# A reordered head: filter loads, the first query tile, evictions and the banks of the first scores

## The chip, the cores and the metric

The kernel runs on 1 core of one Trainium2 chip. The time is what the device takes for one execution of the program, in microseconds (us); a lower time is better. Three runs of the kernel before gave 633.48, 634.38 and 632.29 us, and the profiled execution, a fourth one, took 633.24 us.

## The reference, cut to what matters

Two branches read inputs of their own, and their outputs stand side by side. Branch A is attention with 16 query heads of 28 numbers that share one head of keys and values, over 2048 positions. Branch B is a two-dimensional Fourier filter of a 2048 x 448 array.

```python
def _A_ref(x, wq, wk, wv, wo):
    q = (x @ wq).reshape(B, S, H, Dh).transpose(0, 2, 1, 3)      # H = 16, Dh = 28
    k, v = x @ wk, x @ wv
    scores = jnp.einsum("bhqd,bkd->bhqk", q, k) * (Dh ** -0.5)
    o = jnp.einsum("bhqk,bkd->bhqd", _softmax(scores, axis=-1), v)
    return o.transpose(0, 2, 1, 3).reshape(B, S, H * Dh) @ wo

def _B_ref(x, w_r, w_i):
    X = jnp.fft.rfft2(x, axes=(-2, -1)) * (w_r + 1j * w_i)
    return jnp.fft.irfft2(X, s=(S, D), axes=(-2, -1))

return jnp.concatenate([_A_ref(...), _B_ref(...)], axis=-1)
```

## The kernel before, in words

**Two stages.** The head computes queries, keys and values and the first half of the Fourier transform. The loop after it computes 1024 tiles of scores (128 keys by 512 queries), their exponentials, the sums over values, the output projection, and the rest of the Fourier branch in between.

**The projection in the head.** The input comes in four chunks of 512 positions (`xa` into `raw`). Each number is split into a high part and a remainder, so that fast matmuls keep the precision. `group(n)` (L431) runs the matmuls (L369) of one chunk and one group of heads; the result is copied from PSUM to `qraw` on ScalarE (L373), and VectorE takes its largest magnitude (`qmx`, L374). Four spare rows of each head's 32 carry the keys and values along. `fetch` (L274) gathers the keys into `kf`, `fetch_v` (L280) the values into `vt`.

**The keys.** `keys(h)` makes one half of the key operand `ka`: ScalarE copies the high part (L287), VectorE subtracts it for the remainder `kl` (L288), and three DMAs (L293) fill the other 96 rows: high once more, and the remainder twice. Every score matmul has 128 rows: high and remainder of the query against high and remainder of the key.

**The first query tile.** A score tile needs `qa[0, 0]`. Its chain is: `qmx` times the largest key (`terms`, L296), a small matmul that adds it up per head (`shift`, L301), a copy to `cvec` (L302), the shifted query `ql` (VectorE, L232), its high part `qh` (ScalarE, L229), the remainder (VectorE, L218), and 16 copies `copy_q` of 32 rows each: rows 0 to 31 of the four heads by VectorE (L205), rows 32 to 63 by ScalarE (L203), rows 64 to 95 by DMAs of SP, and rows 96 to 127 by DMAs of POOL (both L206). The first score tile reads head 0, the second head 1, and so on.

**The Fourier half in the head.** For each of eight pieces q, SP loads `xb` (512 KB, L120) and the table `fw` (128 KB, L124). `fft1_fold` (L129 to L134) forms sums on VectorE, `fft1_a` multiplies (L155) and copies out `a` on ScalarE (L144), `fft1_b` multiplies `a` by `fw` (L172), copies the result to `bs` (L180 on ScalarE for q below 6, L182 on VectorE for 6 and 7), and stores it to the DRAM tensor `t1` with two DMAs (`t`, L185). Buffers are reused: the `xb` of piece q + 4 is loaded once `fft1_a(q)` has read it.

**What sets the order.** TensorE, VectorE and ScalarE run in the order of the program text (for the last two from `group(4)` on); SP and POOL issue DMAs in the order shown below. Each engine works through its queue in order. In the loop a table (`PLAN`) and a small clock model choose which instruction comes next. After the head, `free` lists six PSUM banks in the order in which the first scores take them; two banks that the last Fourier piece used and that of the maximum check `pb3` (L503, L504) are among them. From then on a step of the loop is four score tiles (L917), four exponentials (L852 or L928 on ScalarE), and four matmuls with the values (L863).

**After the head.** `fft2_load` (L588) reads `t1` back once all 16 stores have landed, and only behind it on SP's queue come the copies of the second query tile (L223, L225). POOL loads the filter weights `wr`, `wi` (L593).

Of the kernel before, what the change touches and what calls it, by code (L numbers as in the profile page):

```python
# [10 lines left out]
F32 = mybir.dt.float32  # L11
# [4 lines left out]
ALU = mybir.AluOpType  # L16
# [6 lines left out]
DF = D // 2 + 1  # L23
# [49 lines left out]
def kernel(ctx: ExitStack, tc: tile.TileContext, t: dict):  # L73
    nc = tc.nc
# [4 lines left out]
    fp = ctx.enter_context(tc.tile_pool(name="fp", bufs=2))  # L79
# [8 lines left out]
    ka = cp.tile([128, S], F32R, name="ka")  # L88
# [4 lines left out]
    t1 = dp.tile([64, 64, DF], F32, name="t1")  # L93
# [10 lines left out]
    def aux2(name):  # L104
        return aux_pool[0].tile([128, 2, DF], F32, name=name, tag="aux")
# [9 lines left out]
    def fft1_load(q, parts=(0, 1)):  # L115
        if q > 7:
            return
        if 0 in parts:
            x = fp.tile([128, 4, 256], F32, name="xb", tag=("wr", "b2")[q % 2])
            nc.sync.dma_start(x, t["xb"][q])  # L120
            xb[q] = [x, None]
        if 1 in parts:
            w = xb[q][1] = fp.tile([128, 4, 64], F32, name="fw", tag=("ph", "pl")[q % 2])
            nc.sync.dma_start(w, t["fw"][:, 4 * q:4 * q + 4])  # L124

    def fft1_fold(q):
        x = xb[q][0][:113]
        f = fp.tile([113, 4, 256], F32, name="f", tag="wi")
        nc.vector.tensor_tensor(f[:, 0:2], x[:, 0::2], x[:, 1::2], op=ALU.add)  # L129
# [7 lines left out]
    at1, stored = {}, []  # L137

    def fft1_a(*qs):
        for q in qs:  # L140
            for p in range(2):
                pa = fft1_a_mm(q, p)
                a = at1[q, p] = fp.tile([128, 2, DF], F32, name="a", tag=("pwr", "pwi")[p])
                nc.scalar.activation(a, pa, AF.Copy)  # L144
            fft1_load(q + 4, (0,))
# [18 lines left out]
    def fft1_mm(q, pb=None):  # L164
        w = xb[q][1]
        if pb is None:
            pb = aux2("pbb"), ps_o.tile([128, 2, DF], F32, name="po")
        for p in range(2):
            a = at1.pop((q, p))
            for h in range(2):  # L170
                for e in range(2):
                    mm(pb[h][64 * e:64 * e + 64, p], w[64 * h:64 * h + 64, 2 * p + e], a[64 * h:64 * h + 64, e],  # L172
                       start=True, stop=True)
        return pb

    def fft1_out(q, pb):
        bs = fp.tile([128, 2, 2, DF], F32, name="bs", tag="cst" if q < 6 else "b2")
        for h in range(2):
            if q < 6:
                nc.scalar.activation(bs[:, h], pb[h], AF.Copy)  # L180
            else:
                nc.vector.tensor_copy(bs[:, h], pb[h])  # L182
        for e in range(2):
            n0 = 16 * e + 2 * q
            stored.append(nc.sync.dma_start(t1.rearrange("s (l n) f -> s l n f", l=2)[:, :, n0:n0 + 2],  # L185
                                            bs[64 * e:64 * e + 64]))

    def fft2_consts():
        for n in ("g1", "g2"):
# [9 lines left out]
    def copy_q(i, p, q, src, eng):  # L199

        o, x = q[32 * p:32 * p + 32, i], src[32 * i:32 * i + 32].bitcast(F32)
        if eng is nc.scalar:
            return eng.activation(o, x, AF.Copy)  # L203
        if eng is nc.vector:
            return eng.tensor_copy(o, x)  # L205
        return eng.dma_start(o.bitcast(F32), x)  # L206

    def build_q(c, g, first=False):
        cs = slice(c * CW, (c + 1) * CW)
        qh = qp.tile([128, CW], F32R, name="qh", bufs=1)  # L210
        ql = qp.tile([128, CW], F32R, name="ql", bufs=1)
        qt = ql.bitcast(F32)
        if (c, g) not in qa:
            qa[c, g] = qp.tile([128, 4, CW], F32R, name="qa")
        q = qa[c, g]

        def split():
            nc.vector.tensor_tensor(ql, qt, qh.bitcast(F32), op=ALU.subtract)  # L218
# [6 lines left out]
            nc.sync.dma_start(q[64:128].bitcast(F32), q[0:64].bitcast(F32))  # L225

        def high():
            if first:
                return nc.scalar.activation(qh, qt, AF.Copy)  # L229
            return nc.vector.tensor_copy(qh, qt)  # L230

        ops = [(540, lambda: nc.vector.tensor_scalar(qt, qraw[:, g, cs], mask, cvec[:, g, c:c + 1],  # L232
                                                     op0=ALU.mult, op1=ALU.add)),
               (450, high), (710, split)]
        if not first:
            return ops
        for _, op in ops:
            op()
        return q, qh, ql
# [3 lines left out]
    ps_o = ctx.enter_context(tc.tile_pool(name="ps_o", bufs=O_BUFS, space=PSUM))  # L243
# [3 lines left out]
    free = deque(ps_s.tile([128, 512], F32, name=f"s{i}") for i in range(BANKS))  # L247

    def bank():
        free.rotate(-1)  # L250
        return free[-1]

    def pair_of(b):
        return b[:, :2 * DF].rearrange("p (n f) -> p n f", n=2)


    with tc.tile_pool(name="w1", bufs=1) as w1:
# [24 lines left out]
        def keys(h):  # L282
            hs = slice(h * 1024, h * 1024 + 1024)
            kl = w1.tile([32, 1024], F32R, name="kl")
            src = kf[:, hs].rearrange("p (s t j) -> p s t j", s=2, j=32)
            high = ka[:32].rearrange("p (t s j) -> p s t j", s=NC, j=32)[:, 2 * h:2 * h + 2]
            nc.scalar.activation(high, src, AF.Copy)  # L287
            nc.vector.tensor_tensor(kl.rearrange("p (t s j) -> p s t j", s=2, j=32), src, high.bitcast(F32),  # L288
                                    op=ALU.subtract)
            kt = ka.rearrange("p (t x) -> p t x", t=16)[:, :, 64 * h:64 * h + 64]  # L290
            low = kl.rearrange("p (t x) -> p t x", t=16)
            for p, src in ((1, kt[:32]), (2, low), (3, low)):
                nc.sync.dma_start(kt[32 * p:32 * p + 32].bitcast(F32), src.bitcast(F32))  # L293
# [11 lines left out]
        with tc.tile_pool(name="x1", bufs=2) as x1:  # L305
# [151 lines left out]
            for j in range(NK):  # L457
                split_x(*xs[3], 3, j)
            group(5)
            keys(0)  # L460
# [33 lines left out]
        copy_q(1, 1, qf, ql, nc.scalar)  # L494
        fft1_a(6, 7)
# [5 lines left out]
        fft1_b(6, 7)  # L501
        for g in range(NG):
            mm(pb3[0:1, 4 * g:4 * g + 4], cmax[:, g:g + 1], sel4, start=True, stop=True)  # L503
        nc.vector.tensor_reduce(bits, pb3[0:1, 0:16], axis=AX.X, op=ALU.max)  # L504
# [76 lines left out]
    b2 = {}  # L581
# [14 lines left out]
    pr, cst = {}, {}  # L596
# [245 lines left out]
    kept, po = [], {}  # L842
# [341 lines left out]
```

## Time and profile before

| | |
|---|---|
| median of three runs | 633.48 us (632.29 to 634.38) |
| profiled execution | 633.24 us, of which the span from the first to the last instruction is 631.5 us |
| TensorE clock granted | 1.0 over the whole span |
| HBM traffic | 29.77 MB read, 17.87 MB written, 75 GB/s over the span |
| first score matmul | starts 68.17 us after the span's start |
| first exponential of a score | starts at 68.76 us |

The timeline's rows give start, duration, engine (PE is TensorE, DVE VectorE, ACT ScalarE; SPq and POOLq are the issuing queues), line, output and inputs, count, and in brackets the idle time ahead of the row with what ended it. A matmul's record ends some time after the next one has begun, since they are pipelined: 512 columns start 0.23 us apart though one lasts 0.39 us. The time of a DMA row is that of its issue, not of its transfer.

### The profile page before, as it was taken

Reading aid. Unit: us, or ns where it says so; the run is one execution under the profiler, and the core shown is the slowest. Engines: PE = TensorE matmul, PEld = TensorE weight load, DVE = VectorE, ACT = ScalarE, POOL = GpSimd, SP = SyncE. Lnnn points to the kernel's source line nnn. Section 1 sums busy time; section 2 is a strip of 40 time slices with the busy share of each in tenths; the row PEclk is TensorE's granted clock in tenths of the full one; section 3 lists DMA queues with packets and bytes.
Section 4 is the critical chain, followed back from the end, with each engine's and each line's share of the span. In section 5 each row is a group of like instructions: output and inputs, shape, how many; then the busy total and the mean of one; then the engine's idle time right before and its main releaser. Section 6 shows DMA issues by size and latency. Waiting matters only on the chain. (4 is left out here: it accounts for less than half of the span.)

```text
span 631.5 us, 12130 instructions
## 1 busy us (share of the span) xinstructions
PE 625.5 (99%) x4420; PEld 377.6 (60%) x4420; DVE 430.2 (68%) x775; ACT 547.2 (87%) x986; POOL 67.4 (11%) x132
## 2 busy tenths in 40 slices
PE   9999999999999999999999999999999999999997
PEld 7888545655555556646555665555556565555555
DVE  5996458779999944857766845277687764457753
ACT  5565999999999998988899989999989989989991
POOL 3522211011203110000110100001010100000000
PEclk9999999999999999999999999999999999999999
DMA  8857773446456523126340513034152413030001
GB/s 255 290 162 199 215 181 99 103 132 184 121 156 144 149 56 83 59 70 184 80 113 6 128 35 82 16 84 147 42 122 60 111 46 89 16 82 15 17 30 62
DMA packets 40931, 66.71 MB, mean 106 GB/s; under 512 B 11189, under 2 KB 25926, under 8 KB 39904
## 3 DMA queue, kind: packets, MB, share of 16 engines
q1 hardware_dynamic: 35232, 52.50, 30.4%
q0 software_dynamic: 5056, 12.45, 7.6%
q8 instruction: 36, 0.59, 0.4%
q10 hardware_dynamic: 576, 0.92, 0.4%
q14 instruction: 31, 0.25, 0.1%
HBM read 29.77 MB, written 17.87 MB: 75 GB/s over the span
## 5 line engine op out<-in xcount | busy, mean ns | idle before, releaser
L852 ACT ACTIVATE p<-s 128x512 f32<-128x512 f32 x392 | 217.8, 646 | 24.9 <-PE s L917 23.9
L917 PE MATMUL s<-qa,ka 128*128 128x512 f32 x736 | 222.6, 402 | 0.0
L917 PEld LDWEIGHTS s<-qa,ka 128*128 128x128 f32 x736 | 134.5, 188 | 58.6 <-issue 26.2
L863 PE MATMUL s<-p,vs 128*32 128x512 f32 x1144 | 141.7, 595 | 0.0
L923 DVE COPY k<-s 128x512 f32<-128x512 f32 x119 | 78.2, 685 | 68.1 <-PE s L917 67.9
L942 ACT ACTIVATE k<-k 128x1024 f32<-128x1024 f32 x80 | 83.4, 1140 | 0.0
L852 ACT ACTIVATE qraw<-s 128x512 f32<-128x512 f32 x136 | 78.0, 646 | 2.3 <-PE s L917 2.3
L863 PEld LDWEIGHTS s<-p,vs 128*32 128x32 f32 x1144 | 34.3, 109 | 76.2 <-issue 69.7
L852 ACT ACTIVATE p<-po 128x512 f32<-128x512 f32 x88 | 57.2, 650 | 6.5 <-PE po L917 6.4
L917 PE MATMUL po<-qa,ka 128*128 128x512 f32 x151 | 60.9, 404 | 0.0
L917 PE MATMUL sx<-qa,ka 128*128 128x512 f32 x137 | 55.2, 403 | 0.0
L863 PE MATMUL s<-qraw,vs 128*32 128x512 f32 x424 | 54.8, 593 | 0.0
L863 PE MATMUL s<-k,vs 128*32 128x512 f32 x352 | 46.3, 594 | 0.0
L852 ACT ACTIVATE p<-sx 128x512 f32<-128x512 f32 x64 | 42.0, 656 | 3.0 <-PE sx L917 2.9
L738 POOL DMA_DIRECT2D ol<-ol x36 | 18.0, 508 | 229.3 <-DVE ol L761 157.2
L867 DVE STREAM_TRANSPOSE osb<-s 128x512 f32<-128x512 f32 x15 | 10.7, 716 | 38.9 <-PE s L863 38.8
L917 PEld LDWEIGHTS po<-qa,ka 128*128 128x128 f32 x151 | 28.4, 188 | 13.6 <-issue 6.7
L917 PEld LDWEIGHTS sx<-qa,ka 128*128 128x128 f32 x137 | 25.7, 188 | 11.0 <-issue 4.2
L863 PEld LDWEIGHTS s<-qraw,vs 128*32 128x32 f32 x424 | 13.2, 110 | 29.9 <-issue 28.7
L863 PEld LDWEIGHTS s<-k,vs 128*32 128x32 f32 x352 | 11.0, 110 | 25.1 <-issue 24.2
L852 ACT ACTIVATE qraw<-sx 128x512 f32<-128x512 f32 x35 | 22.7, 648 | 2.0 <-PE sx L917 2.0
L923 DVE COPY p<-s 128x512 f32<-128x512 f32 x37 | 24.1, 682 | 0.0
(260 smaller groups left out, 926.2 us busy)
## 6 DMA issues: line engine op xcount, KB each, us to landing
qa<-qa SPq DMA_DIRECT2D x15, 512.0 KB
raw<-xa SPq DMA_DIRECT2D x16, 256.0 KB
xb<-xb SPq DMA_DIRECT2D x8, 512.0 KB
qa<-qh SPq DMA_DIRECT2D x64, 64.0 KB
qa<-ql SPq DMA_DIRECT2D x60, 64.0 KB
t<-bs SPq DMA_DIRECT2D x16, 225.0 KB
wr<-wr POOLq DMA_DIRECT2D x16, 225.0 KB, 3.9
wi<-wi POOLq DMA_DIRECT2D x16, 225.0 KB, 5.1
```

The costliest lines, as they stand in the source:

```text
L738: nc.gpsimd.dma_start(ol[c][o, g].bitcast(F32), ol[c][r, 0].bitcast(F32))
L852: nc.scalar.activation(tiles[-1][:, h % 2], sc, AF.Exp, scale=SCALE)
L863: mm(po[c, g][32 * i:32 * i + 32], vs[:, kc], ps[i // 2][:, i % 2], start=(n == 1), stop=(n == 16))
L867: nc.vector.transpose(o, po[c, g])
L917: begun.append(mm(sc, ka[:, kc * 128:(kc + 1) * 128], qa[c, g][:, h], start=True, stop=True))
L923: nc.vector.tensor_copy(keep[i][h // 2][:, h % 2], sc)
L942: nc.scalar.activation(p, p, AF.Exp, scale=SCALE)
```

## The change

Four edits, all in the head. (1) A piece's stores and the next `fw` load leave `fft1_b` and become `fft1_store`; the two stores of piece 1 now come after `fft1_a(2, 3)`, which issues the loads of `xb` 6 and 7. (2) `keys` returns the remainder's part as `finish`; for the second half it is called after the chain to `qh` and `ql` and after three of the first tile's copies. (3) The copy of head 3's rows 32 to 63 goes from ScalarE to VectorE, the last copy-out of piece 7 (`q + h == 8`) from VectorE to ScalarE, and two copies of `ql` on ScalarE move ahead. (4) The list of banks changes from `a, d, f, e, c, b` to `a, d, f, c, b, e`.

```diff
-    def fft1_b(*qs):
-        for i, q in enumerate(qs):
-            fft1_out(q, fft1_mm(q, [pair_of(bank()) for _ in range(2)] if i else None))
-            fft1_load(q + 4, (1,))
...
+    def fft1_b(q, other=False):
         w = xb[q][1]
...
         for h in range(2):
-            if q < 6:
+            if q < 6 or q + h == 8:
                 nc.scalar.activation(bs[:, h], pb[h], AF.Copy)
             else:
                 nc.vector.tensor_copy(bs[:, h], pb[h])
+
+    def fft1_store(q):
         for e in range(2):
             n0 = 16 * e + 2 * q
...
+        fft1_load(q + 4, (1,))
...
             nc.scalar.activation(high, src, AF.Copy)
...
+            def finish():
+                nc.vector.tensor_tensor(kl.rearrange("p (t s j) -> p s t j", s=2, j=32), src, high.bitcast(F32),
+                                        op=ALU.subtract)
...
+            return finish
...
-            fft1_b(0, 1)
+            fft1_b(0)
+            fft1_store(0)
+            fft1_b(1, True)
             fft1_a(2, 3)
+            fft1_store(1)
...
-            fft1_b(2, 3)
-            keys(1)
+            fft1_b(2)
+            fft1_store(2)
+            fft1_b(3, True)
+            fft1_store(3)
+            finish_keys = keys(1)
             fft1_a(4, 5)
             shift(0, 1)
             qf, qh, ql = build_q(0, 0, True)
+            for i in (0, 1):
+                copy_q(i, 0, qf, qh, nc.vector)
+            copy_q(0, 1, qf, ql, nc.scalar)
+            finish_keys()
             group(11)
             terms(1, NC)
...
         for i in range(4):
             copy_q(i, 2, qf, qh, nc.sync)
+            copy_q(i, 3, qf, ql, nc.gpsimd)
+        for i in (2, 3):
             copy_q(i, 0, qf, qh, nc.vector)
-            copy_q(i, 3, qf, ql, nc.gpsimd)
         fetch_v(range(12, 14), 3)
-        copy_q(0, 1, qf, ql, nc.scalar)
-        fft1_b(4, 5)
         copy_q(1, 1, qf, ql, nc.scalar)
+        fft1_b(4)
...
+        copy_q(2, 1, qf, ql, nc.scalar)
         fft1_a(6, 7)
-        for i in (2, 3):
-            copy_q(i, 1, qf, ql, nc.scalar)
+        copy_q(3, 1, qf, ql, nc.vector)
...
-    free.extend((a, d, f, e, c, b))
+    free.extend((a, d, f, c, b, e))
```

TensorE keeps its instructions and their order; only the names of three banks change. The other engines change at these places. First SP, around the stores of pieces 0 and 1 (`t_72` is `t1`), before:

```order
L293 DMA ka<-kl 32x16x64 x2
L185 DMA t_72<-bs 128x1x450 x2
L124 DMA fw<-fw 128x256
L185 DMA t_72<-bs 128x1x450 x2
L124 DMA fw<-fw 128x256
L120 DMA xb<-xb 128x1024 x2
L274 DMA kf<-qraw 4x1024 x7
```

and with the change:

```order
L289 DMA ka<-kl 32x16x64 x2
L178 DMA t_72<-bs 128x1x450 x2
L124 DMA fw<-fw 128x256
L120 DMA xb<-xb 128x1024 x2
L178 DMA t_72<-bs 128x1x450 x2
L124 DMA fw<-fw 128x256
L268 DMA kf<-qraw 4x1024 x7
```

The two `xb` loads pass two stores and one `fw` load. Next VectorE, from the end of the last fold to the copies of piece 6 and 7, before:

```order
L134 TENSOR_TENSOR xb<-f 113x256
L288 TENSOR_TENSOR kl<-kf,ka 32x2x16x32
L302 COPY cvec<-s_87 128x4
L232 TENSOR_SCALAR ql<-qraw,mask,cvec 128x512
L218 TENSOR_TENSOR ql<-ql,qh 128x512
L374 TENSOR_REDUCE qmx<-qraw 128x1
L296 TENSOR_SCALAR prod<-qmx,kmb 128x4x3
L205 CAST qa<-qh 32x512 x4
L302 COPY cvec<-s_89 128x4x3
```

and with the change:

```order
L134 TENSOR_TENSOR xb<-f 113x256
L299 COPY cvec<-s_87 128x4
L226 TENSOR_SCALAR ql<-qraw,mask,cvec 128x512
L212 TENSOR_TENSOR ql<-ql,qh 128x512
L199 CAST qa<-qh 32x512 x2
L284 TENSOR_TENSOR kl<-kf,ka 32x2x16x32
L371 TENSOR_REDUCE qmx<-qraw 128x1
L293 TENSOR_SCALAR prod<-qmx,kmb 128x4x3
L199 CAST qa<-qh 32x512 x2
L199 CAST qa<-ql 32x512
L299 COPY cvec<-s_89 128x4x3
```

The subtraction that gives `kl` moves behind four steps of the query chain, and a fifth copy joins the four. Last ScalarE, from `qh` to the first exponential (`k<-s_89`), before:

```order
L229 ACTIVATE qh<-ql 128x512
L373 ACTIVATE qraw<-s_88 128x512
L203 ACTIVATE qa<-ql 32x512
L180 ACTIVATE bs<-pbb 128x450
L180 ACTIVATE bs<-po 128x450
L180 ACTIVATE bs<-s_89 128x450
L180 ACTIVATE bs<-s_90 128x450
L203 ACTIVATE qa<-ql 32x512
L144 ACTIVATE a<-s_85 128x450
L144 ACTIVATE a<-s_86 128x450
L144 ACTIVATE a<-s_87 128x450
L144 ACTIVATE a<-s_88 128x450
```

(then two more `qa<-ql` and the exponentials), and with the change:

```order
L223 ACTIVATE qh<-ql 128x512
L197 ACTIVATE qa<-ql 32x512
L370 ACTIVATE qraw<-s_88 128x512
L197 ACTIVATE qa<-ql 32x512
L171 ACTIVATE bs<-pbb 128x450
L171 ACTIVATE bs<-po 128x450
L171 ACTIVATE bs<-s_89 128x450
L171 ACTIVATE bs<-s_90 128x450
L197 ACTIVATE qa<-ql 32x512
L144 ACTIVATE a<-s_85 128x450
L144 ACTIVATE a<-s_86 128x450
L144 ACTIVATE a<-s_87 128x450
```

(then the fourth `a`, `bs<-s_86` and the exponentials). Three copies of `ql` now stand ahead of the `a` copies where two stood; one `bs` copy stands behind them where two copies of `ql` stood. On POOL the four DMAs `qa<-ql` pass one `vt<-qraw`, and the `wr` and `wi` loads follow as before.

More of the change, by code (lines that the diff above doesn't have):

```diff
@@ L135, in fft1_fold @@
         ff[q] = x.rearrange("p k (j h m) -> p k j h m", h=2, m=32)
-    at1, stored = {}, []
+    at1, stored = {}, {}
     def fft1_a(*qs):
@@ L157, in fft1_a_mm @@
         return pa
-    def fft1_b(*qs):
-        for i, q in enumerate(qs):
-            fft1_out(q, fft1_mm(q, [pair_of(bank()) for _ in range(2)] if i else None))
-            fft1_load(q + 4, (1,))
-    def fft1_mm(q, pb=None):
+    def fft1_b(q, other=False):
         w = xb[q][1]
-        if pb is None:
-            pb = aux2("pbb"), ps_o.tile([128, 2, DF], F32, name="po")
+        pb = [pair_of(bank()) for _ in range(2)] if other else (aux2("pbb"), ps_o.tile([128, 2, DF], F32, name="po"))
         for p in range(2):
@@ L173, in fft1_mm @@
                        start=True, stop=True)
-        return pb
-    def fft1_out(q, pb):
-        bs = fp.tile([128, 2, 2, DF], F32, name="bs", tag="cst" if q < 6 else "b2")
+        bs = stored[q] = fp.tile([128, 2, 2, DF], F32, name="bs", tag="cst" if q < 6 else "b2")
         for h in range(2):
-            if q < 6:
+            if q < 6 or q + h == 8:
                 nc.scalar.activation(bs[:, h], pb[h], AF.Copy)
@@ L182, in fft1_out @@
                 nc.vector.tensor_copy(bs[:, h], pb[h])
+    def fft1_store(q):
         for e in range(2):
             n0 = 16 * e + 2 * q
[L185 to L186 removed]
+            stored[-1] = nc.sync.dma_start(t1.rearrange("s (l n) f -> s l n f", l=2)[:, :, n0:n0 + 2],
+                                           stored[q][64 * e:64 * e + 64])
+        fft1_load(q + 4, (1,))
     def fft2_consts():
@@ L287, in keys @@
             nc.scalar.activation(high, src, AF.Copy)
[L288 to L293, printed above, removed]
+            def finish():
+                nc.vector.tensor_tensor(kl.rearrange("p (t s j) -> p s t j", s=2, j=32), src, high.bitcast(F32),
+                                        op=ALU.subtract)
+                kt = ka.rearrange("p (t x) -> p t x", t=16)[:, :, 64 * h:64 * h + 64]
+                low = kl.rearrange("p (t x) -> p t x", t=16)
+                for p, x in ((1, kt[:32]), (2, low), (3, low)):
+                    nc.sync.dma_start(kt[32 * p:32 * p + 32].bitcast(F32), x.bitcast(F32))
+            return finish
         def terms(c0, c1):
@@ L459 @@
             group(5)
-            keys(0)
+            keys(0)()
             group(6)
@@ L488 @@
             copy_q(i, 2, qf, qh, nc.sync)
+            copy_q(i, 3, qf, ql, nc.gpsimd)
+        for i in (2, 3):
             copy_q(i, 0, qf, qh, nc.vector)
-            copy_q(i, 3, qf, ql, nc.gpsimd)
         fetch_v(range(12, 14), 3)
-        copy_q(0, 1, qf, ql, nc.scalar)
-        fft1_b(4, 5)
         copy_q(1, 1, qf, ql, nc.scalar)
+        fft1_b(4)
+        fft1_store(4)
+        fft1_b(5, True)
+        fft1_store(5)
+        copy_q(2, 1, qf, ql, nc.scalar)
         fft1_a(6, 7)
-        for i in (2, 3):
-            copy_q(i, 1, qf, ql, nc.scalar)
+        copy_q(3, 1, qf, ql, nc.vector)
         shift(1, NC)
@@ L500 @@
         pb3 = bank()
-        fft1_b(6, 7)
+        fft1_b(6)
+        fft1_store(6)
+        fft1_b(7, True)
+        fft1_store(7)
         for g in range(NG):
```

## The prediction

> **What bounds the kernel now.** I read the page's busy times first, then the waits of TensorE, then two stretches of the span.
>
> ```profile
> PE 625.5 (99%) x4420; PEld 377.6 (60%) x4420; DVE 430.2 (68%) x775; ACT 547.2 (87%) x986; POOL 67.4 (11%) x132
> PE s L315 <- DVE idle L311: 1.1, 1, 1.1
> PE pbb L172 <- ACT a L144: 0.5, 1, 0.5
> PE s L774 <- DMA oh<-ol: 0.3, 1, 0.3
> 69.00:92.00 23.00, 22.90 (x129) 11.31 (x132) 8.45 (x16) 23.00 (x48) 2.05 (x4) 1.00 0.74 202
> 92.00:600.00 508.00, 507.68 (x3277) 294.46 (x3272) 354.63 (x618) 466.03 (x836) 40.62 (x78) 1.00 0.34 89
> ```
>
> TensorE is named as waiting in three places of the whole span, 1.9 us together, though matmul ends are modelled and waits shorter than a matmul don't show. Of the three the change can touch one, the 0.5 us at L172. The two last rows (stretch, its length, then busy time of PE, PEld, DVE, ACT, POOL) tell what follows the head. From 69 to 92 us ScalarE is busy 23.00 of 23 us, with 48 exponentials at 23/48 = 0.48 us each, so the loop begins at ScalarE's pace. From 92 to 600 us TensorE is busy 507.68 of 508. Neither leaves room for a late start to be made up or an early one to be lost without a new wait. So the change is worth what it moves the first exponential, unless a DMA comes late. The end of the head is this:
>
> ```profile
> 57.26 0.38 PE L301 MATMUL s<-prod,blk 128*128 128x4 f32 x2
> 57.50 0.48 PE L369 MATMUL s<-xh,wqh 128*128 128x512 f32 x1
> 59.88 0.39 PE L369 MATMUL s<-xh,wql 128*128 128x512 f32 x1
> 60.19 0.41 PE L172 MATMUL pbb<-a,fw 64*64 64x225 f32 x2
> 61.00 0.94 PE L172 MATMUL s<-a,fw 64*64 64x225 f32 x16
> 61.87 3.30 PE L155 MATMUL s<-cs,xb 113*32 113x113 f32 x128
> 65.11 0.39 PE L301 MATMUL s<-prod,blk 128*128 128x12 f32 x2
> 66.04 0.41 PE L172 MATMUL pbb<-a,fw 64*64 64x225 f32 x2 [0.54 <-ACT a L144]
> 66.92 1.05 PE L172 MATMUL s<-a,fw 64*64 64x225 f32 x16
> 67.89 0.34 PE L503 MATMUL s<-sel,cmax 128*1 128x4 f32 x8
> 68.17 2.44 PE L917 MATMUL s<-qa,ka 128*128 128x512 f32 x8
> ```
>
> TensorE starts one thing behind the other up to the second `shift` at 65.11. There piece 6 waits for `a`, which ScalarE copies out. The first score follows L503 at 68.17.
>
> **Part 1, the loads.** These rows are SP's and VectorE's.
>
> ```profile
> 43.36 1.03 SPq L124 DMA_DIRECT2D fw<-fw  x1
> 46.93 1.10 SPq L120 DMA_DIRECT2D xb<-xb  x2
> 52.75 0.69 DVE L129 TENSOR_TENSOR f<-xb 113x512 f32<-113x512 f32 x1 [1.62 <-DMA xb<-xb]
> 58.96 1.21 DVE L288 TENSOR_TENSOR kl<-kf,ka 32x1024 fp32r<-32x1024 f32 x1
> 60.10 0.15 DVE L302 COPY cvec<-s 128x4 f32<-128x4 f32 x1
> 60.28 0.55 DVE L232 TENSOR_SCALAR ql<-qraw,mask,cvec 128x512 f32<-128x512 f32 x1
> 61.52 0.69 DVE L218 TENSOR_TENSOR ql<-ql,qh 128x512 fp32r<-128x512 f32 x1 [0.70 <-ACT qh L229]
> 62.99 1.76 DVE L205 CAST qa<-qh 32x512 fp32r<-32x512 f32 x4
> ```
>
> `xb` 6 is issued at 46.93 and holds VectorE up until 52.75. With the change it follows the `fw` load of 43.36 + 1.03 = 44.4, 2.5 us earlier. VectorE is free at 52.75 - 1.62 = 51.13, so the whole idle 1.62 goes if the transfer is early by as much. I take 1.6; the other end is nothing (second rival). The two folds then end at 58.96 - 1.6 = 57.4.
>
> **Part 2, the query chain.** It can't use all of that: `cvec` needs the `shift` on TensorE, done at 57.26 + 0.38 = 57.64. With `kl` out of the way `cvec` is copied at 57.7 and `ql` starts 0.2 later, 57.9, and ends at 58.45, 2.4 us before now. Had part 1 failed, it would be 58.96 + 0.2 = 59.15, still 1.1 us before now.
>
> ```profile
> 56.65 1.80 ACT L144 ACTIVATE a<-s 128x450 f32<-128x450 f32 x4
> 60.86 0.63 ACT L229 ACTIVATE qh<-ql 128x512 fp32r<-128x512 f32 x1 [2.41 <-DVE ql L232]
> 62.25 0.63 ACT L203 ACTIVATE qa<-ql 32x512 fp32r<-32x512 f32 x1 [0.28 <-DVE ql L218]
> 62.90 0.55 ACT L180 ACTIVATE bs<-pbb 128x450 f32<-128x450 f32 x1
> 64.79 0.63 ACT L203 ACTIVATE qa<-ql 32x512 fp32r<-32x512 f32 x1
> 65.44 1.86 ACT L144 ACTIVATE a<-s 128x450 f32<-128x450 f32 x4
> 68.76 4.03 ACT L928 ACTIVATE k<-s 128x512 f32<-128x512 f32 x8
> ```
>
> ScalarE is free at 56.65 + 1.80 = 58.45, so `qh` runs there. VectorE's remainder starts 61.52 - 60.86 = 0.66 later, 59.1, and the first `qa<-ql` 62.25 - 61.52 = 0.73 behind that, 59.85. Then ScalarE adds up: that copy 0.65 (64.79 to 65.44), `qraw` of group 11 (its matmuls end at 60.27, so 60.5 to 61.05), a copy to 61.7, four `bs` 1.89 (62.90 to 64.79) to 63.6, a third copy to 64.25. The four `a` then start at 64.25 and not 65.44. At 1.86/4 = 0.46 each the two of piece 6 are out by 65.25, those of piece 7 by 66.2.
>
> **Part 3, TensorE.** Piece 6 can start 57.50 - 57.26 = 0.24 behind the `shift` at 65.11, so at 65.35 and not 66.04: 0.69 gained. Now it and piece 7 are held a little by `a`, 66.04 to 66.92 to 67.89, 0.88 + 0.97; pieces 4 and 5 did the same work in 61.00 - 60.19 = 0.81 and 61.87 - 61.00 = 0.87. That is 0.17 more. The first score starts at 68.17 - 0.86 = 67.31 and its exponential, 0.59 behind it, at 67.9. ScalarE has its last `bs` copy (0.45 of spacing) to do before that; piece 7 ends near 67.2, so the copy is done by 67.75, just in time. **Sum: -0.86 us.** If ScalarE were late by the whole copy, it would be -0.4.
>
> **What costs nothing, and under what cover.** VectorE ends `kl` at 61.9 (below) and then has a reduction, `terms` and three copies of 1.76/4 = 0.44 to do before the `shift` of 65.11 calls for it again: the fifth copy lies in these 3.2 us, and would cost its 0.44 without them. The bank order: TensorE has given all eight first scores by 68.17 + 2.44 = 70.6, and ScalarE wants the eighth at 68.76 + 7 x 0.48 = 72.1. A bank that is free sooner only lengthens that queue. Were the cover gone, it is what these eight take beyond their pace: 2.44 - 8 x 0.24 (as 57.26 to 57.50) = 0.5 us. The store of piece 1 goes behind two `xb` loads, about 1 us of issuing; its buffer is wanted again by piece 3, whose copy-out comes ahead of the 56.65 row, some ten us later.
>
> **What is late next: `kl`.** It starts behind two copies, at 59.8 + 0.88 = 60.7 and not 58.96, 1.7 us later, and SP stands behind it.
>
> ```profile
> 60.20 1.31 SPq L293 DMA_DIRECT2D ka<-kl  x2
> 61.60 2.50 SPq L206 DMA_DIRECT2D qa<-qh  x4
> 85.06 0.52 SPq L225 DMA_DIRECT2D qa<-qa  x1
> 62.76 2.23 POOL L206 DMA_DIRECT2D qa<-ql  x4
> 65.49 1.04 POOL L593 DMA_DIRECT2D wr<-wr  x2
> DMA to landing us min/median/max: 2.9/3.2/3.4
> DMA to landing us min/median/max: 4.8/5.3/5.8
> ```
>
> The two last rows are the landings of POOL's `qa<-ql` (view of the tile `qa`, 55 to 76 us) and of `wr`, `wi` (view of L593). The four `qa<-qh` move from 61.6 to 63.3 and the last is issued at about 65.2. SP's landings don't stand in the trace. I take the 3.2 us of POOL's copies, of the same shape and size: the first lands at 66.5, before the score at 67.3; the fourth at 68.4. TensorE could use that three scores behind the first, at 67.31 + 3 x 0.31 = 68.2, but ScalarE wants the fourth score only at 67.9 + 3 x 0.48 = 69.35, and 68.4 + 0.59 = 69.0 is in time. Cost: nothing. The far end is the 5.8 us of the weight loads: the first copy then lands at 69.1, its exponential starts at 69.7, and the loop is 69.7 - 68.76 = 0.9 us later than now.
>
> For that end speaks this: POOL's four `qa<-ql` no longer stand behind a `vt` copy that waits for group 11, so they go out from 59.9 to 62.1, and `wr`, `wi`, 225 KB each, start near 63.2 and not at 65.49, in the midst of SP's `qa<-qh`. The Trainium skill, DMA: Bandwidth & Descriptors, section "Queues, rings and completion order", says that each DMA engine takes turns among the queues that have work, a packet at a time, so loads on POOL's queue would slow SP's copies although those were issued by another engine. By that rule the copies come nearer to the far end, and the sum would be +0.9; the profile has no row of an SP landing that would confirm it.
>
> **Rivals.**
>
> *The first query copies land late* (the case above). For it: all copies of SP's part move 1.7 us towards the need while the weight loads move 2.3 us towards them. Against it: now the last copy is issued at 61.60 + 3/4 x 2.50 = 63.5, and no wait of a score for a DMA stands among TensorE's three. Place: the first score. It costs once SP's landing is over 67.31 - 63.3 = 4.0 us, and eats up the whole gain at 4.0 + 0.86 = 4.9; at 5.8 us the time is 633.48 + 0.9 = 634.4, slower than before. It is also what the turns among queues, by the page of the Trainium skill above, would lead to.
>
> *The chain stays where it is.* It needs only part 1 to fail. Then `ql` starts at 59.15, 1.2 us later than in the sum, the first `qa<-ql` at 61.1, and behind it the same five items of ScalarE (0.65 + 0.55 + 0.65 + 1.89 + 0.65 = 4.4) put the `a` copies at 65.5, where they are now: three copies of `ql` ahead of them instead of two eat what `kl` gave up. For it: the landing of `xb` is seen only by the wait that it ends, and the stores behind which it stood may not be what held it. Against it: two stores of 225 KB and a load of 128 KB pass from ahead of it to behind it. Time: 633.5.
>
> *The second query tile comes late.* SP's stores, the reads of them, and the second tile's last copy (issued at 85.06) all stand behind `kl` and move with it.
>
> ```profile
> 94.36 1.43 PE L917 MATMUL s<-qa,ka 128*128 128x512 f32 x5
> ```
>
> TensorE first needs that tile in the scores at 94.36, 93.5 with the change. With 5.8 us of landing it is there at 85.06 + 5.8 + 1.7 = 92.6: 0.9 us to spare. Each us of delay over 1.7 + 0.9 = 2.6 goes into the time; at 5.4 us it would be 633.48 - 0.86 + 2.8 = 635.4. Against it: the stores wait for DMA bandwidth, and earlier `wr` loads leave them more of it.
>
> **How the numbers follow.** The profiled execution of 633.24 us has a span of 631.5; the sum makes it 632.4. It lies 0.24 below the median of the runs, 633.48, and from that the forecast is 632.6; I say 632.7, since the last `bs` copy may cost a tenth. Chances: the forecast 0.58, late first copies 0.17, the chain stays 0.15, a late second tile 0.06, and 0.04 for a wait that I don't see. The three runs lie from 1.2 below to 0.9 above their median; so the low end is 632.7 - 1.2 = 631.5, less 0.3 for the scatter of the other median too, 631.2, and the high end is the first rival's 634.4, which leaves out some 2 in 10. About 0.3% (1.9 us) is what a measurement of this kernel can tell from no change. The forecast is half of that. Faster by more needs a further 1.0 us from the scatter of the runs: a third of the forecast's 0.58, so 0.19. Slower by more: the second tile's 0.06, half of the unseen, and a fifth of the first rival by the same scatter, 0.11. Within: 0.70.
>
> **What would show it.** TensorE's wait for `a` at L172 near 65.5 is gone, VectorE's idle 1.6 before L129 too, `qh` starts near 58.5, the first score near 67.3, the first exponential near 67.9, and the span is shorter by as much. A wait of the first four scores for a DMA would mean the first rival; an idle TensorE or ScalarE near 93 us the third rival. A first exponential that is early with a span as long as before would make the premise wrong that the loop hands an early start on.

## The result: 5 us slower, and the profile after

The change takes 638.32 us (median of 6 runs, 637.35 to 639.33) against 633.19 us before (median of 6, 632.29 to 634.38). The ratio is 1.0079, with a 95% interval of 1.0064 to 1.0094. The forecast was 632.7 us and its range ended at 634.4, so it was wrong in sign and in size. The profiled execution took 638.4 us with a span of 636.6 us, 5.1 us more than the 631.5 us of before. From the page of the change come its busy times and its costliest group of scores:

```profile
PE 625.4 (98%) x4420; PEld 377.9 (59%) x4420; DVE 430.2 (68%) x775; ACT 547.5 (86%) x986; POOL 67.1 (11%) x132
L930 PE MATMUL s<-qa,ka 128*128 128x512 f32 x736 | 223.9, 405 | 4.5 <-DMA qa<-qh 4.5
```

TensorE does the same work in the same 625 us. What is new stands behind the last bar of the second row: 4.5 us in which the scores waited for a DMA. The waits of the change by engine (total, times, longest):

```profile
PE s L930 <- DMA qa<-qh: 4.5, 2, 3.9
...
PE pbb L166 <- ACT a L144: 0.7, 1, 0.7
```

The two waits at L930 have no counterpart before. They stand where the head meets the loop, as the timeline of the change shows:

```profile
64.13 0.39 PE L298 MATMUL s<-prod,blk 128*128 128x12 f32 x2
65.26 0.41 PE L166 MATMUL pbb<-a,fw 64*64 64x225 f32 x2 [0.74 <-ACT a L144]
67.12 0.34 PE L516 MATMUL s<-sel,cmax 128*1 128x4 f32 x8
71.39 0.47 PE L930 MATMUL s<-qa,ka 128*128 128x512 f32 x1 [3.93 <-DMA qa<-qh]
72.47 2.90 PE L930 MATMUL s<-qa,ka 128*128 128x512 f32 x6 [0.61 <-DMA qa<-qh]
56.16 1.06 ACT L281 ACTIVATE ka<-kf 32x1024 fp32r<-32x1024 f32 x1 [1.86 <-DMA kf<-qraw]
58.83 0.61 ACT L223 ACTIVATE qh<-ql 128x512 fp32r<-128x512 f32 x1
64.67 1.86 ACT L144 ACTIVATE a<-s 128x450 f32<-128x450 f32 x4
71.94 0.60 ACT L941 ACTIVATE k<-s 128x512 f32<-128x512 f32 x1 [4.12 <-PE s L930]
73.27 3.04 ACT L941 ACTIVATE k<-s 128x512 f32<-128x512 f32 x6 [0.73 <-PE s L930]
```

TensorE reaches the last step of the head (L516) at 67.12 us, 0.77 us before the 67.89 of the old kernel, and could give the first score at 67.4. It gives it at 71.39 and the second at 72.47. The first exponential runs at 71.94, the second, after another 0.73 us of waiting, at 73.27. What the scores waited for is found in the timeline of VectorE, SP and POOL of the change:

```profile
50.07 0.68 DVE L129 TENSOR_TENSOR f<-xb 113x512 f32<-113x512 f32 x1
60.95 1.21 DVE L284 TENSOR_TENSOR kl<-kf,ka 32x1024 fp32r<-32x1024 f32 x1
62.19 2.16 SPq L289 DMA_DIRECT2D ka<-kl  x2
64.44 2.50 SPq L200 DMA_DIRECT2D qa<-qh  x4
60.46 2.06 POOL L200 DMA_DIRECT2D qa<-ql  x4 [6.46 <-DVE ql L212]
63.57 1.07 POOL L606 DMA_DIRECT2D wr<-wr  x2
64.63 1.03 POOL L606 DMA_DIRECT2D wi<-wi  x2
```

Before, SP issued the `ka<-kl` at 60.20 and the `qa<-qh` at 61.60, and POOL the weights at 65.49 and 66.51. Now SP is 2.0 and 2.8 us later and POOL 1.9 us earlier, so the order has turned round: the weights begin to go out ahead of the `qa<-qh`. By the profile's naming, the first of these copies, issued at 64.44, releases a score at 71.39, 6.95 us later. Three stretches of the change (length, busy time of PE, PEld, DVE, ACT, POOL, granted clock, DMA share, GB/s) show two more things:

```profile
70.00:72.00 2.00, 0.47 (x1) 0.19 (x1) 0.00 (x0) 0.06 (x1) 0.00 (x0) 1.00 1.01 278
72.00:74.00 2.00, 1.53 (x4) 1.27 (x5) 1.12 (x2) 1.27 (x3) 0.00 (x0) 0.61 1.05 364
74.00:76.00 2.00, 2.00 (x9) 1.07 (x11) 0.00 (x0) 2.00 (x5) 0.00 (x0) 0.54 1.01 321
```

The DMA engines are busy all the time (share 1.00), so the copies stood in a crowd, not in an idle machine. Before, the engines were as busy from 66 us on (share 1.00 from 66 to 68), but by then the last query copy had long been issued, by 61.60 + 2.50 = 64.10. And when TensorE starts again, its granted clock is 0.61 and 0.54 in two stretches of 2 us. Before, it was 1.00 in its whole profile.

**The account of the 5.1 us.** A series of exponentials 0.48 us apart that has its second at 73.27 begins at 72.79, which is 4.03 us later than the 68.76 of before. The waits of the scores are 3.93 + 0.61 = 4.54; the head was 0.77 early; an exponential now follows its score 0.80 us (72.47 to 73.27) and not 0.59 us behind, 0.21 more. That gives 3.98 of the 4.03. From there to the end it takes 636.6 - 72.79 = 563.8 us, where before took 631.5 - 68.76 = 562.7. This last 1.1 us falls together with the half clock.

### The profile page after: what moved, and what is told of

Its sections match the earlier page's. It is cut to its first block, busy times and chain, and to the rows that moved or that the text cites. A ratio compares the mean times of both kernels' runs of the same rounds, so it can differ in the third digit from the quotient of the medians.

```text
span 636.6 us, 12130 instructions
## 1 busy us (share of the span) xinstructions
PE 625.4 (98%) x4420; PEld 377.9 (59%) x4420; DVE 430.2 (68%) x775; ACT 547.5 (86%) x986; POOL 67.1 (11%) x132
## 5 line engine op out<-in xcount | busy, mean ns | idle before, releaser
L930 PE MATMUL s<-qa,ka 128*128 128x512 f32 x736 | 223.9, 405 | 4.5 <-DMA qa<-qh 4.5
L930 PEld LDWEIGHTS s<-qa,ka 128*128 128x128 f32 x736 | 135.6, 189 | 62.9 <-issue 26.0
L930 PE MATMUL po<-qa,ka 128*128 128x512 f32 x151 | 61.0, 404 | 0.0
L930 PE MATMUL sx<-qa,ka 128*128 128x512 f32 x137 | 55.3, 404 | 0.0
L930 PEld LDWEIGHTS po<-qa,ka 128*128 128x128 f32 x151 | 28.4, 188 | 13.6 <-issue 6.7
L930 PEld LDWEIGHTS sx<-qa,ka 128*128 128x128 f32 x137 | 25.8, 188 | 11.0 <-issue 4.2
```

The costliest lines, as they stand in the source:

```text
L930: begun.append(mm(sc, ka[:, kc * 128:(kc + 1) * 128], qa[c, g][:, h], start=True, stop=True))
```

## The experiments

Nine kernels were run. Each ratio is to runs of before on the same chip in the same session: 632.64 us (29 runs) for e1 to e4, 631.98 us (8 runs) for e5 to e8, 632.30 us (7 runs) for e9.

**e1: the weights of the first piece wait for a score.** Everything else is as in the change, so `kl` and the copies of SP stand where the change put them.

```diff
-                behind(ld, begun[-1], q == 1)
+                behind(ld, begun[-1], q < 2)
```

> The changed kernel, but POOL's first loads of wr and wi wait for the eighth score (as those of the second piece already wait for a score), so they can no longer run beside SP's copies; ka<-kl and qa<-qh are issued as late as in the change. Theory 'queues meet' (SP's copies land after 6 to 7 us because POOL's 900 KB run on the same DMA engines): the copies land within about 4 us, TensorE's 3.9 us wait for qa<-qh at the first score falls below 1 us, the clock stays at 1.0, and the time is 4 to 5.5 us below the change, about 632.5 to 634. Theory 'too late on SP' (they are late because SP issues them 2 to 3 us later, behind its own stores and remainder): wait and time stay within 1 us of the change, about 638.

Measured: 633.29 us, ratio 1.0015 [1.0003, 1.0027], span 631.8. The timeline of e1:

```profile
62.90 3.53 SPq L200 DMA_DIRECT2D qa<-qh  x4
67.01 2.36 PE L930 MATMUL s<-qa,ka 128*128 128x512 f32 x8
67.60 4.03 ACT L941 ACTIVATE k<-s 128x512 f32<-128x512 f32 x8
69.67 1.07 POOL L606 DMA_DIRECT2D wr<-wr  x2 [6.81 <-PE s L930]
79.19 1.29 SPq L601 DMA_DIRECT2D b<-t  x2
83.92 0.40 DVE L619 CAST bh<-b 128x450 fp32r<-128x450 f32 x1 [13.84 <-DMA b<-t]
85.64 1.33 PE L930 MATMUL s<-qa,ka 128*128 128x512 f32 x4 [1.06 <-DVE k L936]
```

The wait of the first scores is gone, although SP issues its last `qa<-qh` at 66.43, only 0.6 us before the first score. In this execution SP issued its first `qa<-qh` at 62.90 and not at 64.44 as in the change's profile, so e8 below, which issued it at 63.27, is the closer comparison. Together they show that the late issue on SP is not enough to explain the loss; the weights must be there too. The first exponential is 1.16 us earlier than before (68.76), 0.37 us of it because this execution's `shift` ran that much earlier (64.74 for 65.11). But this gain is given back, and the interval lies just above no change: the weights now go out 4.2 us later than before (69.67 for 65.49), in the midst of SP's stores `t<-bs`, the read `b<-t` behind the stores is issued at 79.19 and not at 77.05 as before, VectorE stands in front of it until 83.92 with copies `k` behind, and TensorE waits 1.06 us for these at 85.64. That the weights are what delays the stores is argued from the order; no run tried it alone.

**e2: the keys' remainder back in its place.** The change, with `kl` ahead of the query chain; the weights stay as early as in the change.

```diff
-            finish_keys = keys(1)
+            keys(1)()
...
-            finish_keys()
```

> The changed kernel with the subtraction for kl back ahead of the query chain; loads, copies, evictions, banks and POOL's order stay as changed. Both theories expect the first score's wait to go, since SP issues the copies some 3 us earlier: they are then ahead of the weight loads ('queues meet') and early ('too late on SP'). First score near 67.5 to 68, time 632.3 to 633.5. If the wait stays over 2 us although the copies are issued near 60 us, both are wrong and the cause lies in the loads or in POOL's order.

Measured: 632.65 us, ratio 1.0000 [0.9991, 1.0008], span 630.7. The timeline of e2:

```profile
60.79 2.68 SPq L200 DMA_DIRECT2D qa<-qh  x4
63.53 1.07 POOL L605 DMA_DIRECT2D wr<-wr  x2
67.38 2.22 PE L929 MATMUL s<-qa,ka 128*128 128x512 f32 x8
```

Weights at 63.53 harm nobody when SP's last copy is issued by 63.47. With before and the change, e1 and e2 make a square: early or late copies, early or late weights. Only late copies together with early weights make the first scores wait.

**e4: the loads alone.** Before with the change's first part only: the two `xb` loads pass the store of piece 1.

```diff
...
-            fft1_b(0, 1)
+            store_1 = fft1_b(0, 1, late=True)
             fft1_a(2, 3)
+            store_1()
```

> The kernel before with the first edit alone: the xb loads of pieces 6 and 7 ahead of the stores of piece 1. VectorE's idle 1.6 us ahead of the sixth fold should go in any case. Theory 'the loads give it': the whole chain to the a copies moves up, since kl stays in place and only two copies of ql stand ahead of the a copies; first score 0.5 to 0.9 us earlier, time 632.3 to 632.8 beside 633.2. Rival (the chain is held elsewhere): no change, 633.2 within 0.3. If the loads alone made the copies of the first tile late, it would be slower by 1 us and more.

Measured: 631.98 us, ratio 0.9990 [0.9981, 0.9999], span 630.2. The timeline of e4:

```profile
50.57 0.68 DVE L129 TENSOR_TENSOR f<-xb 113x512 f32<-113x512 f32 x1
64.62 0.39 PE L307 MATMUL s<-prod,blk 128*128 128x12 f32 x2
64.95 0.41 PE L175 MATMUL pbb<-a,fw 64*64 64x225 f32 x2
66.90 2.56 PE L924 MATMUL s<-qa,ka 128*128 128x512 f32 x8
67.49 4.03 ACT L935 ACTIVATE k<-s 128x512 f32<-128x512 f32 x8 [0.69 <-issue]
```

This is the fastest of all kernels run, 0.66 us under before, and its interval just excludes no change. VectorE's idle 1.62 us is gone and so is TensorE's wait for `a`: from the second `shift` to the first score it is 66.90 - 64.62 = 2.28 us, before 68.17 - 65.11 = 3.06, so 0.78 gained.

**e6: the query chain alone.** Before with the change's second part only, so `kl` behind the query chain, and neither the loads nor the evictions nor the banks of the change.

```diff
...
-            keys(1)
+            finish_keys = keys(1)
             fft1_a(4, 5)
             shift(0, 1)
             qf, qh, ql = build_q(0, 0, True)
+            for i in (0, 1):
+                copy_q(i, 0, qf, qh, nc.vector)
+            copy_q(0, 1, qf, ql, nc.scalar)
+            finish_keys()
...
```

> The kernel before with the second edit alone: kl behind the query chain and three copies of the first tile; loads, the copy of head 3, evictions and banks stay. It puts kl later on VectorE and POOL's qa<-ql ahead of the waiting vt copy. Theory (SP's copies come late and POOL's weight loads early, both by this edit): SP's qa<-qh issued near 64 to 66, the weights near 64.5, TensorE waits 2 to 4 us for qa<-qh at the first score, time 636 to 638.5. Rival (it takes the earlier xb loads as well): no wait over 1 us, time 632.5 to 633.5.

Measured: 638.84 us, ratio 1.0114 [1.0092, 1.0136], span 636.9. The timeline of e6:

```profile
64.56 3.06 SPq L206 DMA_DIRECT2D qa<-qh  x4
64.23 1.03 POOL L600 DMA_DIRECT2D wi<-wi  x2
71.91 3.75 PE L924 MATMUL s<-qa,ka 128*128 128x512 f32 x8 [5.33 <-DMA qa<-qh]
```

This part carries the whole loss. Its wait of 5.33 us is longer than the 2 to 4 us expected, and its ratio lies above that of the change, though the two intervals touch (1.0092 and 1.0094).

**e7: the change without its evictions and its bank order.**

```diff
-            if q < 6 or q + h == 8:
+            if q < 6:
...
-        copy_q(2, 1, qf, ql, nc.scalar)
         fft1_a(6, 7)
-        copy_q(3, 1, qf, ql, nc.vector)
+        for i in (2, 3):
+            copy_q(i, 1, qf, ql, nc.scalar)
...
-    free.extend((a, d, f, c, b, e))
+    free.extend((a, d, f, e, c, b))
```

> The changed kernel without the third edit's moves (copy of head 3 back on ScalarE, last copy-out of piece 7 back on VectorE, the third copy behind the a copies) and without the bank order. Theory: these are hidden behind the wait, which stays; time that of the change within 0.5 us, 637.8 to 638.8. Rival (the evictions or the banks are part of the loss): 1 us and more below it.

Measured: 637.99 us, ratio 1.0101 [1.0082, 1.0119], span 636.0. The waits of TensorE in e7:

```profile
PE s L930 <- DMA wi<-wi: 3.0, 1, 3.0
PE s L930 <- DMA qa<-qh: 1.7, 1, 1.7
```

The loss stays, so evictions and banks are not its cause. The first row names `wi`, which the scores don't read. Nor can `wi` have ended this wait: its loads were issued at 64.2 and 64.7 us and landed 6.1 to 7.0 us later by the view of the tile, so not before 70.2, and the score started at 69.53. A wait for several semaphores was put down to the wrong transfer; that it was the first `qa<-qh`, issued at 63.79, is likely but not shown.

**e8: half of the weights.** The change, with only `wi` of the first piece waiting for a score: 450 KB of POOL's loads beside SP's copies and not 900.

```diff
-                behind(ld, begun[-1], q == 1)
+                behind(ld, begun[-1], q == 1 or (q == 0 and n == "wi"))
```

> The changed kernel, but of POOL's first weight loads only the two wr (450 KB) go out early; the two wi wait for the eighth score. Theory 'queues meet': half the bytes beside SP's copies, so the wait at the first score lies between that of e1 (under 0.3) and of the change (3.9), 1 to 2.5 us; time 634 to 636.5. Rival (the first two loads alone do all of it, or it is the order and not the bytes): the wait is as in the change, over 3.3 us, or none.

Measured: 634.53 us, ratio 1.0036 [1.0023, 1.0049], span 633.4. One row of the timeline of e8:

```profile
69.19 3.48 PE L930 MATMUL s<-qa,ka 128*128 128x512 f32 x8 [1.89 <-DMA qa<-qh]
```

No weights, half, all: 0, 1.9 and 4.5 us of waiting (the profiled run of e8 is the slowest of its six, 635.16 us). The loss grows with the bytes that POOL loads.

**e3 and e5: TensorE kept busy ahead of the first score.** The change plus ten (e3) or five (e5) matmuls of 512 columns whose result nobody reads, to see what the half clock costs.

```diff
+    for _ in range(10):
+        mm(a, ident, qraw[:, 0, :CW], start=True, stop=True)
```

> The changed kernel with ten more matmuls (512 columns, their result is never read) ahead of the first score, which fill TensorE's idle 3.9 us. Theory 'clock' (after the idle stretch TensorE runs at about half speed up to 76 us, and that costs 0.5 to 1 us beside the wait): the granted clock stays at 1.0 from 72 to 76 us and the time is 0.5 to 1 us below the change, 637.3 to 637.8. Rival (the wait alone costs it, ScalarE sets the pace behind it): the clock may stay up but the time is that of the change within 0.3 us, or above it if the ten take longer than the wait.

> As e3, with five matmuls of 512 columns in place of ten. In e3 each took 0.86 us and the ten ended 3.4 us after the wait would have; five take 4.3 us, from about 66.5 to 70.8, and leave under 1.5 us of idle. From the first score to the end e3 took 638.1 - 74.8 = 563.3 us, the kernel before 631.5 - 68.2 = 563.3, the change 636.6 - 71.4 = 565.2. Theory 'clock' (the slow clock of 72 to 76 us costs part of these 1.9 us): granted clock 1.0 from 72 to 76, and the time 0.7 to 1.5 us below the change, 636.6 to 637.6. Rival (the 1.9 us are the second to fourth copies, which land 1 to 1.5 us behind the first): the time stays within 0.3 us of the change, 638.0 to 638.6.

Measured: e3 641.08 us, ratio 1.0132 [1.0116, 1.0148], span 638.1; e5 636.40 us, ratio 1.0067 [1.0049, 1.0085], span 634.4. The timeline of e5:

```profile
64.12 0.39 PE L298 MATMUL s<-prod,blk 128*128 128x12 f32 x2
66.13 0.34 PE L516 MATMUL s<-sel,cmax 128*1 128x4 f32 x8
66.40 4.56 PE L530 MATMUL s<-qraw,ident 128*128 128x512 f32 x10
70.39 2.52 PE L932 MATMUL s<-qa,ka 128*128 128x512 f32 x8
71.28 4.03 ACT L943 ACTIVATE k<-s 128x512 f32<-128x512 f32 x8 [4.44 <-PE s L932]
```

Each of these matmuls shows as two records, so the five take 70.39 - 66.40 = 4.0 us and the ten of e3 8.3 (66.55 to 74.84), too long: e3 holds the scores up itself and says nothing of the wait. Both keep the clock at 1.00, and that can be priced from the first exponential to the end: 634.4 - 71.28 = 563.1 us in e5, 638.1 - 75.72 = 562.4 in e3, like the 562.7 of before. In the kernels with the half clock it is 636.9 - 72.76 = 564.1 (e6) and 633.4 - 69.75 = 563.6 (e8), and 563.8 in the change. So against the 562.7 of before the half clock costs about 0.9 to 1.4 us. These are single profiles, and with the clock at 1.00 they spread from 562.4 to 563.1. As a remedy the filler is of little use: e5 stays 4.4 us behind before, and its interval touches that of the change.

**e9: SP's query copies ahead of the keys'.** The change, with the four `qa<-qh` issued ahead of `ka<-kl`.

```diff
             copy_q(0, 1, qf, ql, nc.scalar)
+            for i in range(4):
+                copy_q(i, 2, qf, qh, nc.sync)
             finish_keys()
...
         for i in range(4):
-            copy_q(i, 2, qf, qh, nc.sync)
             copy_q(i, 3, qf, ql, nc.gpsimd)
```

> The change with one move on SP's queue: the four qa<-qh copies are issued ahead of the keys' remainder (kl) instead of behind it, so from about 59.5 us, when qh is there, and not from 64.4. The two ka<-kl copies stay where their data are ready, about 62.2. POOL is as in the change. Theory (an SP copy is slow when it is under way while the 900 KB of wr and wi are): the four qh copies land before the weights start at 63.6 and stop nobody, but the two kl copies are still under way then, land some 6 us after their issue at 62.2 to 63.5, and take the place of the qh copies as what the first score waits for: a wait for ka<-kl of 1 to 2.5 us, first score at 68.3 to 69.8, ratio 1.001 to 1.005, so between the change and before. Rival 1 (the copies are slow because six of them stand in one line on SP): six still stand in one line, so the last of them, now kl's, are as late as qh's were, a wait of about 4 us, ratio 1.008. Rival 2 (only the position behind kl counts, not the weights): no wait of a score for a DMA, first score near 67.2, ratio 0.999 to 1.001.

Measured: 637.85 us, ratio 1.0090 [1.0071, 1.0109], span 635.8. The timeline of e9:

```profile
58.45 2.47 SPq L200 DMA_DIRECT2D qa<-qh  x4
61.70 1.29 SPq L289 DMA_DIRECT2D ka<-kl  x2
63.62 1.03 POOL L607 DMA_DIRECT2D wi<-wi  x2
71.29 3.75 PE L931 MATMUL s<-qa,ka 128*128 128x512 f32 x8 [4.51 <-DMA ka<-kl]
```

The theory had the place right and the size wrong. The `kl` copies, now last, take over the wait as foreseen, and the query copies stop nobody. But they cost 4.5 us, not 1 to 2.5, and the time is the one that the first rival named. That rival, six copies in one line, is out all the same: six stand in that line in e1 and e2 too, and no score waits there. What the theory had missed is the lateness. The second `kl` copy was issued by 61.70 + 1.29 = 62.99, yet a score could start only at 71.29, at least 8.3 us behind it. So there is no fixed landing time, "some 6 us", that begins with the issue. The end of the wait stands against two issues in the kernels where all 900 KB go out (each engine's last row, start plus length):

```
kernel   wait ends   last copy issued (SP)   behind it   last weights issued (POOL)   behind them
change   72.47       66.94                   5.5         65.66                        6.8
e6       71.91       67.62                   4.3         65.26                        6.7
e7       71.95       66.82                   5.1         65.21                        6.7
e9       71.29       62.99                   8.3         64.65                        6.6
```

The distance to SP's own issue lies anywhere from 4.3 to 8.3 us; that to POOL's weights is 6.6 to 6.8. The last of SP's copies that are still under way when the weights begin come about when the weights are through, whenever they themselves were issued. (In e9 the weights landed 6.2 us behind their issue, the last at about 70.3, and the score followed at 71.29.) This holds for the wait that ended last. The change and e7 could start one score before it, at 71.39 and 69.53, which is 5.7 and 4.3 us behind the weights. In e8, with half of the bytes, the wait ends 4.9 us behind the last of the early weights (issued by 64.29).

## Why the prediction was wrong

**The step that failed is "What is late next: `kl`".** It took 3.2 us for SP's landings, from POOL's `qa<-ql`, "of the same shape and size", and concluded: "Cost: nothing". They were 6.95 us for the first query copy, by the profile's naming, and the waits cost 4.54 us. The comparison failed on what ran beside the copies, not on shape or size: in e1, where no weights ran beside them, the first copy was issued at 62.90 and a score read it at 67.01, so it took at most 4.1 us. POOL's `qa<-ql` stood ahead of the weights on the same queue, SP's copies on another queue beside them; that the place in the queue is what spared POOL's copies is argued, not shown. The far end failed for the same kind of reason. It took the weights' own landing of 5.8 us, counted from SP's issue, whereas the last copies come with the end of the weights, whenever they themselves were issued.

**The first rival was the case that came**, with its place and its sign: the first score, the weights that move towards it, slower than before. It had 0.17; the change, e6, e7 and e9, all with late copies and early weights, show its wait. Its price, 634.4, was limited by the 5.8 us. Its own sum with the 6.95 us measured gives a first score at 63.3 + 6.95 = 70.3. The 1.1 us from there to 71.39 lie in SP's issue, at 64.44 and not 63.3: `kl` came 0.25 us later than predicted (60.95 for 60.7), and the two `ka<-kl` ahead took 2.16 us to issue where 1.31 stood before.

The rule that spoke for it was quoted in the prediction and given too little weight. The Trainium skill, DMA: Bandwidth & Descriptors, section "Queues, rings and completion order", has each DMA engine go round the queues that have work, a packet at a time. The queues' shares in the change between 64 and 72 us (packets, MB, share of the 16 engines) show both queues at work in the same stretch:

```profile
q0 software_dynamic: 254, 0.94, 51.6%
q1 hardware_dynamic: 1226, 0.86, 44.5%
```

q0 is POOL's queue and q1 SP's. A packet of POOL's carries 0.94 MB / 254 = 3.7 KB, one of SP's 0.86 MB / 1226 = 0.7 KB, and the two share the engines nearly by half. If the queues took turns packet by packet, the queue with the large packets would gain. The counts do not confirm such turns: nearly five packets of SP's went for each of POOL's (1226 / 254), and SP's count includes the stores issued from 67.03 on. No run here changed the size of packets, so why SP's copies come with the end of the weights is argued and not shown.

That SP's queue is slowed can be read from its packets in single microseconds (the same view). From 63 us on e1 had moved 924 of them by 65 us; the change, whose `ka<-kl` were issued 0.7 us later (62.19 for 61.47), had moved 511 by then and reached 948 only at 67 us. The `qa<-qh` stand behind the `ka<-kl` on that queue, so in the change the first to be held up may be the `kl` copies, which e9 shows as the ones that the score waits for.

**The half clock was not in the sum at all.** Of the miss of 5.1 + 0.86 = 6.0 us it is 1.1, the late copies are the rest.

**The other steps.**
- Part 1, the loads: right. VectorE's wait for `xb` is gone in the change and in e4.
- Part 2, the query chain: right in its bounds, since `ql` starts 0.2 us behind `cvec` (56.90 in the change) and `qh` when ScalarE is free. But the prediction counted the loads and the query chain as one gain. The wait for `a` is gone in e4, which has the loads alone, and also in e6, which has the chain alone; with the loads made, the chain had nothing left to earn, and only its cost remained. For the same reason the second rival, by which the chain needs the loads, was priced wrongly: in e6 the `a` copies run at 63.48, and the third copy ahead of them that the change has (0.65 us) would put them at 64.1 by estimate, still ahead of the `shift` at 64.23.
- Part 3, TensorE: right, though the profile of the change seems to deny it. There 0.74 us of the wait for `a` stay, because ScalarE got to `ka<-kf` only at 56.16, after 1.86 us of waiting for `kf` (0.40 before), and the `a` copies behind it ran at 64.67 and not at 64.25, although this execution's `shift` was 0.98 us early. In none of the nine experiments is TensorE named as waiting there, and e1, e3, e5 and e8 have the change's head as it is. Their waits ahead of `ka<-kf` lie between none (e1) and 1.32 us (e8), so the late `kf` is put down to this one execution. In e5 it is 66.13 - 64.12 = 2.01 us from the `shift` to L516, before 67.89 - 65.11 = 2.78: 0.77 us gained, where the sum had 0.86. The 0.77 us by which the change's own profile ends the head early are another matter: its `shift` already ran 0.98 us early.
- The bank order and the fifth copy "cost nothing": not contradicted. e7, without them, loses like the change. e2, which has them and the loads, is level with before, but its interval overlaps e4's; they were not tried alone.
- The premise that the loop hands a late start on held: of the 5.1 us, 4.0 are the start of the exponentials, and the rest falls together with the half clock.
- The third rival did not come: no score near 93 us waited.

## What to carry to other kernels

When a step moves a small copy later, look at what the other queues begin to load by then, and price the copy as landing behind those loads; a landing time read from copies that ran ahead of such a load says nothing. When two parts of a change are meant to remove the same wait, cost each alone: here the one that moved only loads brought all of the gain, and the other removed the same wait at a price far above it. A large load that nobody needs soon can stand behind the small ones that somebody waits for, but look at what it then meets, as the stores in e1.

## What the runs showed of the hardware

- **The granted clock falls after short waits.** It stood at 0.61 and 0.54 (72 to 76 us) after the change's wait of 3.93 us. In e8 a wait of 1.89 us was enough. Two stretches of e8, and two of e6:

```profile
70.00:72.00 2.00, 2.00 (x6) 1.61 (x6) 1.12 (x2) 2.00 (x5) 0.00 (x0) 0.57 0.90 284
72.00:74.00 2.00, 2.00 (x10) 0.20 (x8) 0.00 (x0) 1.82 (x4) 1.03 (x2) 0.58 0.82 259
...
68.00:70.00 2.00, 0.00 (x0) 0.00 (x0) 0.92 (x2) 0.00 (x0) 0.00 (x0) 0.75 1.02 218
70.00:72.00 2.00, 0.09 (x1) 0.12 (x1) 0.00 (x0) 0.00 (x0) 0.00 (x0) 0.50 0.99 280
```

  Where the wait is short, the clock falls only when TensorE is busy again: in e8 from 70.3 us on, the scores having begun at 69.19. In e6, with its wait of 5.33 us, it falls during the wait. Read in windows of 0.25 us, the clock is 1.00 or 0.50 but for the edges: 0.50 for 3.4 us in the change (72.4 to 75.8) and in e8 (70.3 to 73.7), and for 6.8 us in e6 (69.0 to 75.8), e7 (69.4 to 76.2) and e9 (69.2 to 76.0). The Trainium skill, TensorE: Matmul & The Clock Gate, section "Part 1: The HAM clock gate (the "warmup" mystery)", names an idle window of about 3.4 us as the condition. The change's wait agrees with that, and so does the length of the slow stretches, once or twice 3.4 us; e8's wait, which is shorter, does not by itself. What TensorE did ahead of e8's wait (small matmuls, 1.30 us busy in the 2 us up to 68) may count as idle; no run tells.
- **The start of the head scatters.** TensorE's `shift` near 64 to 65 us ran at 65.11 before, 64.13 in the change, 64.62 in e4 and 64.74 in e2. The difference is there already in the first matmuls: the first single `xh,wqh` matmul starts at 7.21, 6.27, 6.74 and 6.88 us, and the `shift` 57.9 us behind each. Two profiled spans must be compared from a point inside the head, or by the medians.
